# Decay and bonus tables spread by a rank-one product, a reordered first pair, and 3 KB output rows in an RWKV-5 plus soft-MoE kernel

## The chip, the core and the metric

The kernel runs on one core of a Trainium2 chip. Five engines share the work: TensorE multiplies matrices (in the profile PE, and PEld for its weight loads), VectorE (DVE) and ScalarE (ACT) work elementwise and can read what TensorE leaves in PSUM, GpSimd (POOL) works elementwise on SBUF and issues some DMAs, SyncE (SP) issues most DMAs. Each engine executes its own queue in order and waits for the others by semaphores. The metric is device time in microseconds (us), the median of several runs; lower is better. The profile covers a span about 2 us shorter than the device time.

## What is computed

Two stages, one after the other. The first is a linear attention with a decaying state, for 4 batches, 8 heads, 768 steps and head size 48; the second is a soft mixture of 8 experts with 4 slots each, over the 3072 tokens that the first produces (8 heads x 48 = 384 channels):

```python
for t in range(S):
    kt, vt, rt = (k[:, :, t], v[:, :, t], r[:, :, t])
    cur = np.einsum('bhd,bhe->bhde', u[None] * kt, vt)
    y[:, :, t] = np.einsum('bhd,bhde->bhe', rt, state + cur)
    state = w[None, :, :, None] * state + np.einsum('bhd,bhe->bhde', kt, vt)
...
logits = x @ phi                      # x: 3072 x 384, phi: 384 x 32
d = softmax of logits over tokens;  c = softmax of logits over slots
slot_out[e] = relu((d.T @ x)[e] @ w1[e]) @ w2[e]
out = c @ slot_out                    # 3072 x 384, float32
```

`w` (the decay per head and channel, 0.85 to 0.95) and `u` (the bonus for the step itself) have 8 x 48 = 384 values each.

## The kernel before

**Tiling.** The 3072 tokens are cut into 12 blocks of 256, called pairs because each holds two chunks of 128 steps. A block is loaded as `r_l`, `k_l`, `v_l`, each 128 partitions x 8 heads x 2 neighbouring steps (J = 2) x 48. Partitions 0 to 63 hold the first chunk, 64 to 127 the second. In DRAM each run of a load is 2 x 48 x 4 = 384 bytes. The pool `ld` has four buffers of each, so loads run ahead of the work, all on SP's queue, in the order k, r, v (line 70).

**The decay tables.** Within a chunk the decay is taken out of the recurrence by scaling r with `W_n = w^(step-128)` and k with `W_k = w^(127-step)`, both tables of 128 x 768 float32. Before: DMAs spread `w` and `u` over all 128 partitions (`w_rep` line 82, `u_rep` line 75; the latter sits behind the first `k_l` in SP's queue), ScalarE takes the logarithm of `w_rep` (line 122) and two exponentials (123, 124), VectorE makes the other two halves by a product with `w_rep` (125, 126). Behind these products, in VectorE's queue, stand 13 memsets of constants and of the padding of `rr` and `kk` (129 to 143). Separately `w_pd` collects `w` with channels on partitions, by two DMAs of 4-byte elements issued from ACT's queue; GpSimd squares it seven times to get `w^128` (line 148), and `tables()` spreads it into `wm`, which the state update multiplies by.

**A pair.** `mults(n)` makes `rr = r * W_n`, `kk = k * W_k` (bfloat16) and `ku = k * u` (float32): on GpSimd for n > 0; for n = 0 `ku` on GpSimd, `rr` and `kk` on VectorE (lines 191 to 193). `trans` transposes `rr` or `kk` by eight TensorE products into the single PSUM tile `t_p`, which ScalarE copies out. `att(n, j)` multiplies them to attention scores (two PSUM tiles `at_p0`, `at_p1`), VectorE masks them into `at_s` (line 261). The diagonal term is r.(u k): ScalarE copies r into the PSUM tile `rp` (`r_copy`), VectorE multiplies `ku` by it (`kur`, line 219), sums (226) and scales v (`dv`, 228); `diag` is the last two. `y_open`, `inter`, `intra` gather the output of the pair in PSUM, `state` and `st_next` advance the state, `x_copy` takes the output out. Two iterations behind, `xt`, `lg`, `expo`, `disp` compute the logits, their exponentials and the slots' inputs; every second iteration `lexp_t` transposes the exponentials into `LexpT`, and `rowsum` sums them per token into `rsum_r`. `rp` is one PSUM buffer, so the second `r_copy` of a pair waits for the first `kur`.

**Order.** It is written out by hand. Ahead of the loop (lines 405 to 415) stand `mults(0)`, the transposes of pair 0 (`rr` first), the diagonal of pair 0, and `mults(1)`. Iteration n of the loop (line 416) computes attention and state of pair n while preparing pair n + 1 and issuing `load(n + 3)` and, on GpSimd, `mults(n + 2)` and then one load of expert weights (`load_w`, 16 of 768 KB as stored; seven of them follow the last `mults`). After the loop come the experts (`up`, `down`) and the output stage (lines 501 to 517): for each of 12 blocks two products of 32 x 128 weights with 384 columns, one result scaled by VectorE and one by ScalarE into `o_s`, and one DMA. There a partition holds one row of each of two 128-token groups, so a run in DRAM is one row, 1536 bytes.

Of the kernel before, what the change touches and what calls it, by code (L numbers as in the profile page):

```python
# [11 lines left out]
def kernel(  # L12
# [12 lines left out]
    nc = tc.nc  # L25
    B, H, S, D = r.shape
    C = 128
    nC = S // C
    Nn, Dm = out.shape
    assert Nn == B * S and Dm == H * D  # L30
    ES = moe_phi.shape[1]
# [11 lines left out]
    P = 128  # L43
# [21 lines left out]
    def load(n):  # L65
        if n >= nS:
            return
        b, i = divmod(n, nSb)
        loads[n] = [ld.tile([P, H, J, D], f32, name=name) for name in ("r_l", "k_l", "v_l")]
        for x, src in ((1, k), (0, r), (2, v)):  # L70
            t = loads[n][x]
            nc.sync.dma_start(out=t[:].rearrange("p h j d -> p h (j d)"),
                              in_=src[b, :, i * TS:(i + 1) * TS, :].rearrange("h (p j) d -> p h (j d)", j=J))
            if n == 0 and x == 1:
                nc.sync.dma_start(out=u_rep[:].rearrange("p h d -> p (h d)"),
                                  in_=u.flatten().partition_broadcast(P))

    def jh(t):
        return t[:].rearrange("p h j d -> p j h d")

    w_rep = cst.tile([P, H, D], f32, name="w_rep")
    nc.sync.dma_start(out=w_rep[:].rearrange("p h d -> p (h d)"), in_=w.flatten().partition_broadcast(P))
    u_rep = cst.tile([P, H, D], f32, name="u_rep")
    w_pd = cst.tile([P, nP], f32, name="w_pd")
    nc.vector.memset(w_pd[:], 1.0)
    for par in range(2):
        nc.scalar.dma_start(out=w_pd[par * 64:par * 64 + D, :],
                            in_=w.rearrange("(q a) d -> a d q", a=2)[par])
# [6 lines left out]
    for a in range(2):  # L95
# [7 lines left out]
    row = cst.tile([P, J], f32, name="row")  # L103
    nc.vector.tensor_copy(row[:, 0:1], row_i[:])
    nc.vector.tensor_scalar_add(row[:, 1:2], row[:, 0:1], 1.0)
    ex_n = cst.tile([P, 1], f32, name="ex_n")
    nc.vector.tensor_scalar_add(ex_n[:], row[:, 0:1], float(-C))
    ex_k = cst.tile([P, 1], f32, name="ex_k")
    nc.vector.tensor_scalar(out=ex_k[:], in0=row[:, 1:2], scalar1=-1.0, scalar2=float(C - 1),
                            op0=ALU.mult, op1=ALU.add)  # L110
    col_f = cst.tile([P, J, HF], f32, name="col_f")
    nc.vector.tensor_copy(col_f[:], col_i[:])
# [2 lines left out]
        nc.vector.tensor_scalar(out=mask[:, j, :], in0=col_f[:].rearrange("p j c -> p (j c)"),  # L115
                                scalar1=row[:, j:j + 1], scalar2=None, op0=ALU.is_gt)

    W_n = cst.tile([P, J, H, D], f32, name="W_n")
    W_k = cst.tile([P, J, H, D], f32, name="W_k")
    logw = cst.tile([P, H, D], f32, name="logw")  # L120
    nc.scalar.activation(out=warm[:], in_=warm[:], func=AF.Ln)
    nc.scalar.activation(out=logw[:], in_=w_rep[:], func=AF.Ln)
    nc.scalar.activation(out=W_n[:, 0, :, :], in_=logw[:], func=AF.Exp, scale=ex_n[:])
    nc.scalar.activation(out=W_k[:, 1, :, :], in_=logw[:], func=AF.Exp, scale=ex_k[:])
    nc.vector.tensor_mul(W_n[:, 1, :, :], W_n[:, 0, :, :], w_rep[:])
    nc.vector.tensor_mul(W_k[:, 0, :, :], W_k[:, 1, :, :], w_rep[:])

    ones = cst.tile([P, P], bf, name="ones")
    nc.vector.memset(ones[:], 1.0)
    blk = cst.tile([P, G], bf, name="blk")  # L130
    nc.vector.memset(blk[:], 0.0)
    for q in range(G):
        nc.vector.memset(blk[q * ES:(q + 1) * ES, q:q + 1], 1.0)
    wm = cst.tile([P, nP, D2], f32, name="wm")
    nc.vector.memset(wm[:], 0.0)
    phi_s = cst.tile([P, nM, ES], bf, name="phi_s")
# [8 lines left out]
    st_t = [cst.tile([P, nP, D2], bf, name=f"st{i}") for i in range(2)]  # L145

    for _ in range(C.bit_length() - 1):
        nc.gpsimd.tensor_mul(w_pd[:], w_pd[:], w_pd[:])

    def tables():  # L150
        for par in range(2):
# [26 lines left out]
    with tc.tile_pool(name="wk", bufs=2) as wk, \  # L178
         tc.tile_pool(name="wk3", bufs=3) as wk3, \
         tc.tile_pool(name="ps", bufs=1, space=bass.MemoryType.PSUM) as ps:  # L180
        sc = {}

        def mults(n):
            if n >= nS:
                return
            r_l, k_l, v_l = loads[n]
            rr, kk = rr_t[n % NB], kk_t[n % NB]
            ku = wk.tile([P, J, H, D], f32, name="ku")
            u_b = u_rep[:, None, :, :].to_broadcast([P, J, H, D])
            if n == 0:  # L190
                nc.gpsimd.tensor_mul(ku[:], jh(k_l), u_b)
                nc.vector.tensor_mul(rr[:, :, :, 0:D], jh(r_l), W_n[:])  # L192
                nc.vector.tensor_mul(kk[:, :, :, 0:D], jh(k_l), W_k[:])  # L193
            else:
                nc.gpsimd.tensor_mul(rr[:, :, :, 0:D], jh(r_l), W_n[:])  # L195
                nc.gpsimd.tensor_mul(kk[:, :, :, 0:D], jh(k_l), W_k[:])  # L196
                nc.gpsimd.tensor_mul(ku[:], jh(k_l), u_b)  # L197
            sc[n] = dict(rr=rr, kk=kk, ku=ku)
# [8 lines left out]
        def r_copy(n, j):  # L207
            if n >= nS:
                return
            s = sc[n]  # L210
            if j == 0:
                s["rp"] = ps.tile([P, H, D], f32, name="rp")
            nc.scalar.copy(s["rp"][:], jh(loads[n][0])[:, j, :, :])  # L213

        def kur(n, j):
            if n >= nS:
                return
            s = sc[n]
            nc.vector.tensor_mul(s["ku"][:, j, :, :], s["ku"][:, j, :, :], s["rp"][:])  # L219

        def diag(n):
            if n >= nS:
                return
            s = sc[n]
            d = s["rp"][:].rearrange("p h d -> p (h d)")[:, 0:J * H].rearrange("p (j h) -> p j h", j=J)
            nc.vector.tensor_reduce(d, s["ku"][:], axis=mybir.AxisListType.X, op=ALU.add)  # L226
            dv = wk.tile([P, J, H, D], bf, name="dv")
            nc.vector.tensor_mul(dv[:], s["v"][:], d[:, :, :, None].to_broadcast([P, J, H, D]))  # L228
            s["dv"] = dv

        def trans(n, nm):
            if n >= nS:
                return
            s = sc[n]
            t_p = ps.tile([P, nP, 2, J, HF], bf, name="t_p")
            for q in range(nP):
                for j in range(J):
                    nc.tensor.transpose(t_p[:, q, :, j, :],  # L238
                                        s[nm][:, j, 2 * q:2 * q + 2, :].rearrange("p h d -> p (h d)"), ident[:])
            t_s = wk.tile([P, nP, 2, J, HF], bf, name=f"t_{nm}")  # L240
            nc.scalar.copy(t_s[:], t_p[:])  # L241
            s["t_" + nm] = t_s
# [149 lines left out]
        def lexp_t(g):  # L392
            le_p = ps.tile([P, P + 2 * G], bf, name="le_p", tag="xl_p", padded_shape=[P, XW + 4 * ES])
            lt_of[g] = le_p
            nc.tensor.transpose(le_p[:, 0:P], le_of[g][:].rearrange("p g s -> p (g s)"), ident[:])
            nc.scalar.copy(LexpT[:, g, :].rearrange("s (p j) -> s j p", j=J),
                           le_p[:, 0:P].rearrange("s (j p) -> s j p", j=J))

        def rowsum(g):
            rs_p = lt_of.pop(g)[:, P:P + 2 * G].bitcast(f32)  # L400
            nc.tensor.matmul(rs_p, LexpT[:, g, :], blk[:], start=True, stop=True, skip_group_check=True)
            nc.vector.reciprocal(rsum_r[:, g * G:(g + 1) * G], rs_p)

        W_AT = [1, 1, 1, 1, 1, 1, 1, 1, 1, 1, 2, 2, 1, 1]
        mults(0)
        trans(0, "rr")
        r_copy(0, 0)
        trans(0, "kk")
        v_cast(0)
        tables()  # L410
        kur(0, 0)
        r_copy(0, 1)
        kur(0, 1)
        diag(0)
        mults(1)
        for n in range(nS + 2):
            live = n < nS
            load(n + 3)
            group = (n - 3) // 2 if n >= 3 and n % 2 == 1 else None
            att(n, 0)  # L420
            mults(n + 2)
            s_now = ps.tile([P, nP * D2], f32, name="s_p")
            disp(n - 2, s_now)
# [74 lines left out]
                                soT[:, mi, :, :].rearrange("p g s -> p (g s)"), ident[:])  # L498
        nc.vector.tensor_copy(so_r[:], sr_p[:])

    out_ap = out.rearrange("(no p) m -> p no m", p=P)
    with tc.tile_pool(name="ob", bufs=6) as ob, \
         tc.tile_pool(name="out_ps", bufs=2, space=bass.MemoryType.PSUM) as out_ps:
        for g in range(nG):
            for jj in range(0, G, 2):
                o_s = ob.tile([P, 2, Dm], f32, name="o_s")
                for j in (jj, jj + 1):
                    o_p = out_ps.tile([P, Dm], f32, name=f"o_p{j}")
                    nc.tensor.matmul(o_p[:], LexpT[j * ES:(j + 1) * ES, g, :], so_r[j * ES:(j + 1) * ES, :],  # L509
                                     tile_position=(j * ES, 0))  # L510
                    ni = g * G + j
                    if j % 2 == 0:
                        nc.vector.tensor_scalar_mul(o_s[:, 0, :], o_p[:], rsum_r[:, ni:ni + 1])
                    else:
                        nc.scalar.activation(out=o_s[:, 1, :], in_=o_p[:], func=AF.Copy,  # L515
                                             scale=rsum_r[:, ni:ni + 1])
                nc.sync.dma_start(out=out_ap[:, g * G + jj:g * G + jj + 2, :], in_=o_s[:])


# [28 lines left out]
```

The softmax here doesn't subtract the row's maximum and nothing guards it: scores larger than these inputs give would overflow.

## Time and profile before

Device time 147.52 us (median of 3 runs, 147.45 to 148.28); the profiled span is 145.3 us. The stages, as the table of stretches and the order of instructions give them:

| stretch, us | what runs | length, us |
|---|---|---|
| 0 to 20.47 | loads, tables, first pair, until VectorE masks the first scores | 20.5 |
| 20.47 to 105.4 | the first 11 of the 12 iterations, each from one masking of `att(n, 0)` to the next | 84.9 |
| 105.4 to 116.7 | the last iteration, logits and slots of the last pairs | 11.3 |
| 116.7 to 128.3 | the experts | 11.6 |
| 128.3 to 145.3 | output | 17.0 |

Over the whole span VectorE and TensorE are busy 66%, GpSimd 54%, ScalarE 52%. Such shares average stages with different limits, so they say little about what an edit at the start or at the end is worth; the views by stage in the prediction say more.

How to read the lines there: a line of the order of instructions (the timeline) gives start, length, engine, source line, operation, output <- inputs, shape and count, and in brackets the idle time of the engine just ahead and what ended it. A line of stretches gives the stretch, its length, each engine's busy time and count of instructions, the TensorE clock that was granted, the mean busy share of the 16 DMA engines (transfers that overlap can bring it above 1) and GB/s moved. SPq, ACTq are the queues that issue DMAs.

### The profile page before, as it was taken

To read this page: it belongs to the slowest core of one execution; us is meant where nothing else is said; L and a number is where in the kernel's file an instruction comes from. 1 tells how busy PE (TensorE), PEld (TensorE's weight loads), DVE (VectorE), ACT (ScalarE), POOL (GpSimd) and SP (SyncE) were. 2 spreads that over 40 slices of the span, in tenths; PEclk is the share of its full clock that TensorE was granted. 3 is DMA by queue.
4 is the path that set the end of the run, shared out by engine and by line. 5 is a ranking of instruction groups with operands and counts; after the bars stand their busy time and mean duration, and the time that the engine had idled before them with its cause. 6 is when DMAs were issued, how large, how long until landed. Compare 5 with 4: busy or idle time off the path is not lost.

```text
span 145.3 us, 4488 instructions
## 1 busy us (share of the span) xinstructions
PE 95.6 (66%) x1927; PEld 73.2 (50%) x1927; DVE 96.0 (66%) x191; ACT 75.4 (52%) x123; POOL 77.9 (54%) x67
## 2 busy tenths in 40 slices
PE   0004509998858996858489994799767489977000
PEld 0004306777636865646357873676646289931000
DVE  3095197979888679998988688868980223267600
ACT  4713833657776648584958277763914300046500
POOL 5195999895998398999591899940000000000000
PEclk9999999999995559999975589555995555555555
DMA  3999999999999999999999949699999990009995
GB/s 58 230 301 324 321 320 312 185 261 206 306 240 241 238 262 228 228 287 229 252 234 239 260 55 196 98 201 210 205 208 208 206 188 11 5 26 361 367 362 189
DMA packets 52980, 32.19 MB, mean 221 GB/s; under 512 B 38352, under 2 KB 49872, under 8 KB 52960
## 3 DMA queue, kind: packets, MB, share of 16 engines
q0 software_dynamic: 11552, 12.63, 52.7%
q1 hardware_dynamic: 40992, 19.27, 47.1%
q8 instruction: 15, 0.25, 0.6%
q10 hardware_dynamic: 416, 0.00, 0.2%
q14 instruction: 5, 0.04, 0.1%
HBM read 39.77 MB, written 4.72 MB: 306 GB/s over the span
## 4 chain that ended last, share of the span: by engine, by line
PE 34%; DVE 22%; ACT 19%; DMA 13%; issue 7%; SPq 0%; ACTq 0%; DVEq 0%
DVE at_s L261 11%; PE at_p L256 6%; DMA out_dram<-o_s 5%; DMA r_l<-in_r_dram 5%; ACT t_kk L241 4%; DVE ku L219 4%; PE t_p L238 4%; PE h_p L470 4%; ACT xt_s L346 4%; PE so_p L482 4%; PE xl_p L344 3%; PE s_p L301 3%; ACT v_bf L204 3%; DMA w_rep<-in_w_dram 3%; ACT x_t L330 2%
## 5 line engine op out<-in xcount | busy, mean ns | idle before, releaser
L261 DVE TENSOR_TENSOR at_s<-at_p,mask 128x512 bf16<-128x512 f32 x48 | 30.9, 686 | 10.0 <-PE at_p L256 9.9
L196 POOL TENSOR_TENSOR kk<-k_l,W_k 128x768 bf16<-128x768 f32 x11 | 19.9, 1810 | 11.3 <-PE s_p L301 10.7
L195 POOL TENSOR_TENSOR rr<-r_l,W_n 128x768 bf16<-128x768 f32 x11 | 20.0, 1821 | 1.9 <-DVE kk L193 1.7
L241 ACT COPY t_rr<-t_p 128x1024 bf16<-128x1024 bf16 x12 | 12.1, 1012 | 16.1 <-PE t_p L238 16.1
L197 POOL TENSOR_TENSOR ku<-k_l,u_rep 128x768 f32<-128x768 f32 x11 | 20.0, 1816 | 0.0
L256 PE MATMUL at_p<-t_rr,t_kk 64*64 64x128 bf16 x384 | 15.0, 264 | 7.3 <-DVE at_s L261 6.2
L213 ACT COPY rp<-r_l 128x384 f32<-128x384 f32 x24 | 11.6, 485 | 15.2 <-DVE ku L219 13.6
L238 PE MATMUL t_p<-ident,rr 128*128 128x128 bf16 x96 | 9.8, 263 | 11.8 <-DVE rr L192 11.8
L219 DVE TENSOR_TENSOR ku<-ku,rp 128x384 f32<-128x384 f32 x24 | 13.2, 550 | 5.5 <-ACT rp L213 4.9
L515 ACT ACTIVATE o_s<-o_p,rsum_r 128x384 f32<-128x384 f32 x12 | 6.4, 585 | 16.3 <-PE o_p L509 13.8
L256 PEld LDWEIGHTS <-t_kk 64*64 64x64 bf16 x384 | 9.3, 128 | 10.7 <-issue 8.1
L176 POOL DMA_DIRECT2D w_all<-in_moe_w_dram x16 | 13.6, 854 | 0.0
L238 PEld LDWEIGHTS <-rr 128*128 128x128 bf16 x96 | 7.3, 118 | 12.1 <-DVE rr L192 11.8
L301 PE MATMUL s_p<-v_bf,kk 64*128 64x96 bf16 x160 | 13.3, 240 | 0.0
L301 PEld LDWEIGHTS <-kk 64*128 64x128 bf16 x160 | 9.7, 113 | 5.8 <-issue 5.8
L241 ACT COPY t_kk<-t_p 128x1024 bf16<-128x1024 bf16 x12 | 12.1, 1006 | 0.9 <-PE t_p L238 0.7
L228 DVE TENSOR_TENSOR dv<-v_bf,rp 128x768 bf16<-128x768 bf16 x12 | 11.4, 954 | 1.2
L310 DVE TENSOR_TENSOR st<-s_p,wm 128x384 bf16<-128x384 f32 x20 | 11.1, 553 | 1.7 <-PE s_p L301 1.5
L330 ACT CAST x_t<-y_p 128x768 bf16<-128x768 f32 x12 | 9.7, 805 | 4.5 <-PE y_p L323 4.3
L226 DVE TENSOR_REDUCE rp<-ku 128x16 f32<-128x768 f32 x12 | 11.5, 958 | 0.3
L346 ACT COPY xt_s<-xl_p 128x768 bf16<-128x768 bf16 x12 | 9.6, 800 | 3.7 <-PE xl_p L344 3.6
L238 PE MATMUL t_p<-ident,kk 128*128 128x128 bf16 x96 | 9.9, 265 | 1.1 <-ACT t_rr L241 1.1
(78 smaller groups left out, 175.7 us busy)
## 6 DMA issues: line engine op xcount, KB each, us to landing
w_all<-in_moe_w_dram POOLq DMA_DIRECT2D x16, 768.0 KB, 10.1
k_l<-in_k_dram SPq DMA_DIRECT2D x12, 384.0 KB, 6.7
r_l<-in_r_dram SPq DMA_DIRECT2D x12, 384.0 KB, 8.0
v_l<-in_v_dram SPq DMA_DIRECT2D x12, 384.0 KB, 7.4
out_dram<-o_s SPq DMA_DIRECT2D x12, 384.0 KB, 4.1
w_rep<-in_w_dram SPq DMA_DIRECT2D x1, 192.0 KB, 3.9
u_rep<-in_u_dram SPq DMA_DIRECT2D x1, 192.0 KB, 6.0
phi_f<-in_moe_phi_dram POOLq DMA_DIRECT2D x1, 48.0 KB, 5.9
```

The lines of the kernel that those rows point to most:

```text
L176: nc.gpsimd.dma_start(out=dst[:, e, :, :], in_=src[:, e, :, :])
L195: nc.gpsimd.tensor_mul(rr[:, :, :, 0:D], jh(r_l), W_n[:])
L196: nc.gpsimd.tensor_mul(kk[:, :, :, 0:D], jh(k_l), W_k[:])
L197: nc.gpsimd.tensor_mul(ku[:], jh(k_l), u_b)
L219: nc.vector.tensor_mul(s["ku"][:, j, :, :], s["ku"][:, j, :, :], s["rp"][:])
L238: nc.tensor.transpose(t_p[:, q, :, j, :], s[nm][:, j, 2 * q:2 * q + 2, :].rearrange("p h d -> p (h d)"), ident[:])
L241: nc.scalar.copy(t_s[:], t_p[:])
L256: nc.tensor.matmul(at_p[a][g * HF:(g + 1) * HF, q, :], kT[sl, q, g, j, :], rT[sl, q, g, :, :].rearrange("p j c -> p (j c)"), start=True, s ...
L261: nc.vector.tensor_mul(s["at"][:, a, j, :, :], at_p[a][:], mask[:, j, None, :].to_broadcast([P, nP, P]))
L301: nc.tensor.matmul(s_p[:, q * D2:(q + 1) * D2], s["kk"][sl, j, 2 * q:2 * q + 2, :].rearrange("p h d -> p (h d)"), s["v"][sl, j, 2 * q:2 * ...
L330: nc.scalar.copy(x_t[:], sc[n]["y"][:, :, 0:Dm])
L346: nc.scalar.copy(xt_s[:], xl_p[:, 0:XW])
```

## The change

Four groups of edits, shortened to their core:

1. **Tables.** `w` and `u` come as one row each (1.5 KB) instead of 128 copies. The logarithm is taken of one row; a product with a row of ones on TensorE (float32, contraction length 1) spreads log w and u over the partitions, into the PSUM buffers that `att` uses later. All four halves of the tables are exponentials read from PSUM, `W_k` first; VectorE copies `u_rep` from PSUM. The products of lines 125 and 126 are gone, and the memsets no longer stand behind them.
2. **First pair.** VectorE makes `kk`, `rr` and `ku` of pair 0, in this order; the squarings of `w_pd` move from GpSimd to VectorE, ahead of them. k is transposed first. Pair 0 has a PSUM buffer of its own for the first r copy, so both copies can go early. The sum of the diagonal comes ahead of the transposes, its product with v (`dmul`) after the first `att`. `mults(1)` is put into GpSimd's queue ahead of the transposes.
3. **Row sums.** `LexpT` keeps the even and odd steps apart; `rowsum` becomes four small products.
4. **Output.** A partition holds two neighbouring tokens, so a run in DRAM is 3 KB; a block takes four products of 32 x 64 weights instead of two of 32 x 128.

```diff
-            if n == 0 and x == 1:
-                nc.sync.dma_start(out=u_rep[:].rearrange("p h d -> p (h d)"),
-                                  in_=u.flatten().partition_broadcast(P))
...
-    w_rep = cst.tile([P, H, D], f32, name="w_rep")
-    nc.sync.dma_start(out=w_rep[:].rearrange("p h d -> p (h d)"), in_=w.flatten().partition_broadcast(P))
+    wu_row = cst.tile([1, 2, Dm], f32, name="wu_row")
+    for t, src in enumerate((w, u)):
+        nc.sync.dma_start(out=wu_row[:, t, :], in_=src.flatten()[None, :])
...
-    nc.scalar.activation(out=logw[:], in_=w_rep[:], func=AF.Ln)
-    nc.scalar.activation(out=W_n[:, 0, :, :], in_=logw[:], func=AF.Exp, scale=ex_n[:])
-    nc.scalar.activation(out=W_k[:, 1, :, :], in_=logw[:], func=AF.Exp, scale=ex_k[:])
-    nc.vector.tensor_mul(W_n[:, 1, :, :], W_n[:, 0, :, :], w_rep[:])
-    nc.vector.tensor_mul(W_k[:, 0, :, :], W_k[:, 1, :, :], w_rep[:])
...
     for _ in range(C.bit_length() - 1):
-        nc.gpsimd.tensor_mul(w_pd[:], w_pd[:], w_pd[:])
+        nc.vector.tensor_mul(w_pd[:], w_pd[:], w_pd[:])
...
+        nc.scalar.activation(out=logw[:], in_=wu_row[:, 0, :], func=AF.Ln)
+        lw_p = ps.tile([P, Dm], f32, name="lw_p", tag="at_p0", padded_shape=[P, nP * P])
+        u_p = ps.tile([P, Dm], f32, name="u_p", tag="at_p1", padded_shape=[P, nP * P])
+        nc.tensor.matmul(u_p[:], ones_f[:], wu_row[:, 1, :], start=True, stop=True)
+        nc.tensor.matmul(lw_p[:], ones_f[:], logw[:], start=True, stop=True)
+        for Wt, ex in ((W_k, ex_k), (W_n, ex_n)):
+            for j in range(J):
+                nc.scalar.activation(out=Wt[:, j, :, :].rearrange("p h d -> p (h d)"), in_=lw_p[:], func=AF.Exp,
+                                     scale=ex[:, j:j + 1])
+        nc.vector.tensor_copy(u_rep[:].rearrange("p h d -> p (h d)"), u_p[:])
...
             if n == 0:
-                nc.gpsimd.tensor_mul(ku[:], jh(k_l), u_b)
+                nc.vector.tensor_mul(kk[:, :, :, 0:D], jh(k_l), W_k[:])
                 nc.vector.tensor_mul(rr[:, :, :, 0:D], jh(r_l), W_n[:])
-                nc.vector.tensor_mul(kk[:, :, :, 0:D], jh(k_l), W_k[:])
+                nc.vector.tensor_mul(ku[:], jh(k_l), u_b)
...
-            nc.tensor.matmul(rs_p, LexpT[:, g, :], blk[:], start=True, stop=True, skip_group_check=True)
+            for q2 in range(2):
+                for j in range(J):
+                    nc.tensor.matmul(rs_p[q2 * HF:(q2 + 1) * HF, 2 * j:2 * j + 2],
+                                     LexpT[:, g, j * HF:(j + 1) * HF], blk[:, q2, :],
+                                     start=True, stop=True, tile_position=(0, q2 * HF), skip_group_check=True)
...
         mults(0)
+        r_copy(0, 0)
+        r_copy(0, 1)
+        kur(0, 0)
+        kur(0, 1)
+        dsum(0)
+        mults(1)
+        trans(0, "kk")
         trans(0, "rr")
-        r_copy(0, 0)
-        trans(0, "kk")
         v_cast(0)
         tables()
-        kur(0, 0)
-        r_copy(0, 1)
-        kur(0, 1)
-        diag(0)
-        mults(1)
...
             att(n, 0)
+            if n == 0:
+                dmul(0)
             mults(n + 2)
...
-    out_ap = out.rearrange("(no p) m -> p no m", p=P)
+    out_ap = out.rearrange("(i p j) m -> i p j m", p=P, j=J)
...
-                    nc.tensor.matmul(o_p[:], LexpT[j * ES:(j + 1) * ES, g, :], so_r[j * ES:(j + 1) * ES, :],
-                                     tile_position=(j * ES, 0))
+                for q2 in range(2):
+                    q = 2 * qh + q2
+                    nc.tensor.matmul(o_p[q2 * HF:(q2 + 1) * HF, :],
+                                     LexpT[q * ES:(q + 1) * ES, g, j * HF:(j + 1) * HF],
+                                     so_r[q * ES:(q + 1) * ES, :],
+                                     tile_position=(q * ES, q2 * HF), skip_group_check=True)
```

## The prediction

> **What bounds the kernel now.** I read three views: the order of instructions at the start, the stretches of the loop, and the output stage.
>
> The start, to the first masking of scores on VectorE:
>
> ```profile
> 0.74 0.39 SPq L82 DMA_DIRECT2D w_rep<-in_w_dram  x1
> ...
> 4.69 0.52 ACT L122 ACTIVATE logw<-w_rep 128x384 f32<-128x384 f32 x1 [1.38 <-DMA w_rep<-in_w_dram]
> 5.23 1.28 ACT L123 ACT_TABLE_LOAD   x1
> ...
> 6.72 2.41 POOL L148 TENSOR_TENSOR w_pd<-w_pd 128x4 f32<-128x4 f32 x7 [3.88 <-DMA w_pd<-in_w_dram]
> 7.18 0.56 DVE L125 TENSOR_TENSOR W_n<-W_n,w_rep 128x384 f32<-128x384 f32 x1 [4.81 <-ACT W_n L123]
> ...
> 9.07 1.81 POOL L191 TENSOR_TENSOR ku<-k_l,u_rep 128x768 f32<-128x768 f32 x1
> ...
> 10.06 1.64 DVE L192 TENSOR_TENSOR rr<-r_l,W_n 128x768 bf16<-128x768 f32 x1
> 11.63 0.95 DVE L193 TENSOR_TENSOR kk<-k_l,W_k 128x768 bf16<-128x768 f32 x1
> ...
> 12.59 1.81 POOL L195 TENSOR_TENSOR rr<-r_l,W_n 128x768 bf16<-128x768 f32 x1 [1.71 <-DVE kk L193]
> ...
> 18.01 0.55 DVE L219 TENSOR_TENSOR ku<-ku,rp 128x384 f32<-128x384 f32 x1 [3.13 <-ACT rp L213]
> ...
> 20.47 1.28 DVE L261 TENSOR_TENSOR at_s<-at_p,mask 128x512 bf16<-128x512 f32 x2
> ```
>
> VectorE sits idle 4.8 us until the tables, then does 13 memsets (8.2 to 10.1), and scales r before k. Pair 0's scores exist at 16.6, but their masking waits until 20.47: the second r copy stands behind four ScalarE operations (17.50), and the diagonal behind it. GpSimd begins pair 1 at 12.59 because r_l of pair 1, issued at 7.69, took 4.8 us to land (the DMA view); the releaser named is a guess.
>
> The loop:
>
> ```profile
> 58.50:65.70 7.20, 5.12 (x127) 3.97 (x124) 6.24 (x12) 5.33 (x10) 7.18 (x5) 1.00 1.20 258
> ...
> 72.90:82.00 9.10, 8.39 (x133) 6.38 (x133) 6.80 (x13) 5.60 (x10) 5.47 (x4) 0.58 1.17 237
> 82.00:89.40 7.40, 5.57 (x124) 4.31 (x122) 6.17 (x10) 5.07 (x9) 7.38 (x6) 0.82 0.85 150
> ```
>
> Columns: stretch, length, busy time of PE, PEld, DVE, ACT, POOL, clock, DMA share, GB/s. At full clock an iteration lasts 7.2 us with VectorE busy 6.2; at half clock PE takes over (8.4 of 9.1). This happens in three iterations (8.8, 9.1, 8.5). The loop hangs on engines, not loads: the r_l of pair 11 lands at 84.0, yet its transpose runs near 98.5. So a start x earlier should move the loop by x, while loads keep up.
>
> The output:
>
> ```profile
> 132.00:134.00 2.00, 1.18 (x6) 0.20 (x4) 1.38 (x3) 1.17 (x3) 0.00 (x0) 0.50 1.00 363
> 134.00:136.00 2.00, 0.50 (x2) 0.10 (x1) 1.06 (x2) 1.05 (x2) 0.00 (x0) 0.50 1.00 363
> ```
>
> DMA is full (share 1.00, 363 GB/s), the engines have time: 12 x 393 KB at 363 GB/s is 13.0 of the 17 us.
>
> [...] No float32 product is in this trace. [...] The 1536-byte packets here gave 363 GB/s. [...]
>
> **Part by part.**
>
> *DMA ahead of the loads.* Removed: 2 x 196 KB. k_l landed at 7.1 (1.19 + 5.9), r_l at 8.9, v_l at 10.1, then one per 1.2 us. In the new order k_l is issued about 1.6, with two 1.5 KB rows ahead. w_rep's transfer began about 1 us after issue, 393 KB at 300 GB/s takes 1.3, landing adds 1: k_l about 5.0, r_l 6.2, v_l 7.5, pair 1's k_l 8.7, r_l 9.9. Gain 2.1 to 2.7 us; certainly over 1.2, the removed bytes at 320 GB/s.
>
> *Tables.* The rows land about 2.2 us after issue (the smallest DMA time in the trace is 2.5; bounds 1.8 and 4), w at 2.9. The logarithm follows the table load and warm-up (3.31) and lasts 0.52: 3.8. TensorE makes u first. [...] u from 3.3 to 4.8, log w to 6.3. The second table load (1.28) hides beside them. Four exponentials of 0.6 (L123): W_k ready at 7.5, W_n at 8.7 (bounds 5.5 and 10).
>
> *VectorE before kk.* The memsets (about 2 us) now lie in its idle time, before 5. The squarings add a wait: w_pd landed at 6.54, now with less traffic 5.3 to 6.5, then seven dependent operations of 0.15 (row L105), 1.05; then the u copy, 0.5 (VectorE's 384-column rows: 0.36 to 0.62). Everything of pair 0 on VectorE is queued behind that wait, and TensorE waits for kk. Free at 6.9 to 8.1; kk starts at 7.8. On GpSimd nothing useful goes away: 4.2 us lay before 12.59 anyway.
>
> *Pair 0.* kk 7.8 to 8.75, rr to 9.7, ku to 10.65 (0.95 each, L193). [...] Two kur at 0.55 and the sum at 0.96, as before: VectorE free at 13.0. Meanwhile: k transposes 8.75 to 9.8 (8 in 1.03), copy to 10.8 (1.01); t_p is one buffer, so r's transposes follow, to 11.9, copy to 13.0; att 0.64, scores at 13.6. Masking starts at 13.9 instead of 20.47: 6.6 us. The product dmul (0.95), formerly ahead of it, now stands behind: the second masking comes at 13.9 + 1.28 + 0.95 = 16.1 instead of 22.48. Gain 6.3 us. [...]
>
> *Carried through the loop?* GpSimd is only 2 to 2.5 us earlier: pair 1 from 10.6 to 16.0, pair 2 to 21.4 (3 x 1.81 each). ku of pair 2 is needed at 23.7 - 6.3 + 7.3 = 24.7: in time. It needs 3 x 1.81 + 0.8 = 6.2 us of an iteration of 7.2. Loads gain 2.4, not 6.3, as DMA is full (share over 1.0) to 84; their lead of over 10 us shrinks by 4. The last expert load lands at 120.9 and is used about 126.5. Loads have 1.7 us of DMA work less, and the dip of 82 to 89.4 (share 0.85, 150 GB/s) holds some 3 us; GpSimd issues the tail's seven loads after its last pair, so the last lands about 117 against a need at 120.2. So all 6.3 are carried; a half-clock iteration more or less is 1.3 to 1.9 either way.
>
> *Row sums.* 18 more products of 0.2 us over six groups, mostly in gaps of PE; the last group stands before the experts: +0.1. Unstrided LexpT copy: under 0.05, nothing.
>
> *Output.* [...] I take 0.2. The first block needs two more products: +0.1. Later ones hide behind the DMA: evictions take 0.62 of 1.08 per block.
>
> Sum: -6.3 + 0.1 - 0.2 + 0.1 = -6.3; 147.5 - 6.3 = 141.2 us.
>
> **Rivals.**
>
> [...]
>
> *DMA sets the end.* If loads or the expert tail move only with the removed bytes (2.4 us), 145.1. For it: DMA shares over 1.0. Against: the dip and the 5.6 us of slack.
>
> *Output gains more, or a half-clock phase goes:* 139.
>
> [...]
>
> **How the numbers follow.** Forecast 0.55, part lost 0.22, more 0.12, DMA 0.08, slower 0.03. Time: 141.2. The range leaves out the slow case, most of the DMA case and the edges: 138.3 to 144.3. Within 1% means 146.0 to 149.0: only mixtures of the DMA case and a worse start, 0.04. Slower 0.03, faster 0.93.
>
> **What would show it.** r_l of pair 1 landing near 9.9; W_k from 6.3 to 7.5; VectorE's kk at 7.8 and not behind w_pd past 8.1; first masking near 13.9; iterations of 7.2 to 9.1 as before; the experts 6.3 us earlier, without a wait for their weights; output DMA at 363 to 375 GB/s. Wrong it would be if the iterations lengthened to the DMA's pace, if the float32 products took over 2 us each, or if PE showed up as the releaser of every output eviction.

## The result and the profile after

Device time fell from 147.8 us (4 runs, 147.45 to 148.28) to **140.91 us** (4 runs, 140.58 to 142.17): a ratio of 0.955, 95% interval 0.948 to 0.961. The profiled span fell from 145.3 to 139.2 us. On another chip the same kernel gave 142.48 us beside 147.58 (ratio 0.962, 0.956 to 0.968). Single runs on some chips were disturbed; the ratios leave them out, the medians don't, and two kernels below (the old order and the combined one) were profiled in such a run, so that little but their start is read.

The 6.17 us of span, by stage; a stage ends where the next begins, and minus means shorter:

| stage ends with | before, us | after, us | this stage alone |
|---|---|---|---|
| first masking on VectorE | 20.47 | 13.00 | -7.47 |
| masking of the last pair (loop) | 105.40 | 97.42 | -0.51 |
| slots of all tokens done | 116.61 | 108.69 | +0.06 |
| experts' result (`so_r`) | 128.33 | 122.57 | **+2.16** |
| end | 145.34 | 139.17 | -0.41 |

So the start gave 7.5 us and the loop kept it. The experts lost 2.2 us, and the output gave 0.4.

The start, from the order of instructions of the kernel after:

```profile
3.04 1.61 PE L180 MATMUL u_p<-wu_row,ones_f 1*128 1x384 f32 x2 [3.04 <-DMA wu_row<-in_u_dram]
...
3.75 1.28 ACT L184 ACT_TABLE_LOAD   x1
...
4.26 1.29 DVE L138 TENSOR_TENSOR w_pd<-w_pd 128x4 f32<-128x4 f32 x7
4.45 1.48 PE L181 MATMUL lw_p<-logw,ones_f 1*128 1x384 f32 x2
...
5.97 1.05 ACT L184 ACTIVATE W_k<-lw_p,ex_k 128x384 f32<-128x384 f32 x2 [0.94 <-PE lw_p L181]
...
7.05 0.96 DVE L196 TENSOR_TENSOR kk<-k_l,W_k 128x768 bf16<-128x768 f32 x1 [1.04 <-ACT W_k L184]
...
8.87 0.95 DVE L198 TENSOR_TENSOR ku<-k_l,u_rep 128x768 f32<-128x768 f32 x1
...
10.43 1.80 POOL L200 TENSOR_TENSOR rr<-r_l,W_n 128x768 bf16<-128x768 f32 x1 [7.51 <-DMA r_l<-in_r_dram]
...
12.32 0.64 PE L274 MATMUL at_p<-t_rr,t_kk 64*64 64x128 bf16 x16 [1.10 <-ACT t_rr L259]
...
13.00 1.29 DVE L279 TENSOR_TENSOR at_s<-at_p,mask 128x512 bf16<-128x512 f32 x2 [1.06 <-PE at_p L274]
```

`kk` starts at 7.05 instead of 11.63, and the bracket names what holds it now: the exponentials of W_k, not the squarings (over at 5.55) or `k_l` (landed at 5.07). The masking now waits for the scores themselves (`<-PE at_p`); before, it stood in VectorE's queue behind the diagonal. The reads of `t_kk` and `t_rr` out of `t_p` and the scores form a chain of TensorE and ScalarE alone.

The loop and the output, as stretches (columns as before: stretch, length, busy PE, PEld, DVE, ACT, POOL, clock, DMA share, GB/s):

```profile
27.75:34.94 7.19, 4.82 (x121) 3.80 (x122) 6.17 (x10) 5.14 (x9) 7.15 (x6) 1.00 1.15 262
34.94:43.68 8.74, 7.97 (x130) 6.12 (x130) 6.76 (x12) 5.42 (x10) 8.72 (x6) 0.55 1.23 250
...
81.27:90.00 8.73, 8.26 (x130) 6.35 (x130) 6.76 (x12) 5.35 (x9) 7.69 (x6) 0.50 0.87 140
...
130.00:132.00 2.00, 0.00 (x0) 0.00 (x0) 1.28 (x3) 1.21 (x3) 0.00 (x0) 0.50 1.01 397
```

Eight of the eleven iterations last 7.2 to 7.5 us and three, at a clock of 0.50 to 0.61, 8.1 to 8.7; before, there were three such too, of 8.5 to 9.1. The last line is new: a full DMA moves 397 GB/s at the output, where it moved 363.

The experts:

```profile
113.32 0.78 PE L493 MATMUL h_p<-unsiT,w_all 128*128 128x4 bf16 x24
...
113.96 0.78 PE L505 MATMUL so_p<-hT,w_all 128*128 128x4 bf16 x24
...
114.60 0.25 PE L493 MATMUL h_p<-unsiT,w_all 128*128 128x4 bf16 x4
...
116.53 0.69 PE L493 MATMUL h_p<-unsiT,w_all 128*128 128x4 bf16 x20 [1.68 <-issue]
...
119.64 0.46 PE L505 MATMUL so_p<-hT,w_all 128*128 128x4 bf16 x12
120.25 1.12 PE L505 MATMUL so_p<-hT,w_all 128*128 128x4 bf16 x36 [0.16 <-issue]
```

The 24 products of a layer follow at 0.027 us each (0.64 us from one layer to the next). In the sixth expert TensorE stops after 4 of 24, and again 128 products later, after 12 of 24. The brackets name no engine and no DMA: `issue` is time in which the profile shows nothing that the engine waits for. Counted from where the next product was due (114.60 + 4 x 0.027 = 114.71, and 119.64 + 12 x 0.027 = 119.96), the holes are 1.82 and 0.29 us: together 2.1 of the 2.16 us lost. The loss varies: in a second profile of the same kernel (experiment 6) the holes stand at the same places and come to 1.84 and 1.12 us, and the experts took 14.72 us instead of 13.88. The last expert weights landed at 118.33, so a wait for data was the first suspect.

### The profile page after: what moved, and what is told of

Same layout as the page of the kernel before. It is cut to its first block, busy times and chain, and to the rows that moved or that the text cites. A ratio compares the mean times of both kernels' runs of the same rounds, so it can differ in the third digit from the quotient of the medians.

```text
span 139.2 us, 4595 instructions
## 1 busy us (share of the span) xinstructions
PE 101.7 (73%) x1973; PEld 77.1 (55%) x1973; DVE 96.6 (69%) x199; ACT 76.1 (55%) x125; POOL 74.2 (53%) x59
## 4 chain that ended last, share of the span: by engine, by line
PE 42%; ACT 21%; DVE 18%; issue 8%; DMA 6%; SPq 0%; ACTq 0%; DVEq 0%
DVE at_s L279 10%; PE at_p L274 6%; PE t_p L256 6%; ACT t_kk L259 5%; DMA out_dram<-o_s 5%; PE h_p L493 4%; PE xl_p L362 4%; DVE ku L228 4%; PE so_p L505 4%; ACT xt_s L364 4%; PE s_p L319 3%; ACT v_bf L209 3%; ACT x_t L348 3%; PE y_p L341 2%; ACT rp L222 2%
## 5 line engine op out<-in xcount | busy, mean ns | idle before, releaser
L200 POOL TENSOR_TENSOR rr<-r_l,W_n 128x768 bf16<-128x768 f32 x11 | 19.9, 1813 | 18.5 <-DMA r_l<-in_r_dram 18.4
L228 DVE TENSOR_TENSOR ku<-ku,rp 128x384 f32<-128x384 f32 x23 | 12.6, 548 | 0.7
L256 PE MATMUL t_p<-ident,kk 128*128 128x128 bf16 x96 | 10.4, 273 | 2.1 <-DVE kk L196 2.1
L239 DVE TENSOR_REDUCE rp<-ku 128x16 f32<-128x768 f32 x12 | 11.5, 958 | 0.3
L256 PEld LDWEIGHTS <-kk 128*128 128x128 bf16 x96 | 7.7, 123 | 4.6 <-DVE kk L196 3.3
```

The costliest lines, as they stand in the source:

```text
L256: nc.tensor.transpose(t_p[:, q, :, j, :], s[nm][:, j, 2 * q:2 * q + 2, :].rearrange("p h d -> p (h d)"), ident[:])
```

## Experiments

The edits are shown in short; some lines only name what changes.

**1. Which group pays: the start alone, and the output alone.** The first kernel has groups 1 and 2 with the old row sums and output; the second has groups 3 and 4 on the start of before.

```diff
 # start alone: the kernel after with (in words)
+rs_p = LexpT[:, g, :] x blk              (one product per group, not four)
+out_ap = out.rearrange("(no p) m -> p no m", p=P)     (1536-byte runs)
```

> Groups 1 and 2 of the change alone; row sums and output as before. Theory: the start carries the whole gain up to the experts (first masking at 13.0 as in the changed kernel against 20.5 before, logits done 7.9 us earlier), and the experts then lose up to 2.2 us to a stall, so 139.6 to 141.8 us; the output stage lasts 17.0 us at 363 GB/s. Rival: the 3 KB rows earn a good part of the 6.9 us, then this kernel stays at 143 or above.

> Groups 3 and 4 of the change alone; start as before. Theory: the output DMA runs at 397 instead of 363 GB/s, 1.1 us less of transfer, of which 0.4 to 0.8 is lost because the first block is issued later; first masking at 20.5; 146.7 to 147.3 us. Rival: the rows are worth their full 1.1 us or more, 146.4 or below, or the four small products per block hold the DMA back, 148 or above.

The start alone took 143.06 us (beside 147.07; ratio 0.967, 0.953 to 0.981), with the first masking at 12.71. The output alone took 146.9 us (ratio 1.002, 0.997 to 1.006): its output stage was 0.42 us shorter, 16.59 instead of 17.01, but this is 0.3% and disappears in the interval of the whole. The gain is that of the start.

The total of the start alone lies where the rival expected it (143 or above), but not for the rival's reason: the start gave 7.8 us, as the theory has it, and the experts lost 4.3, not up to 2.2.

The start alone showed more of the experts (16.02 us instead of 11.72):

```profile
113.68 0.73 PE L490 MATMUL h_p<-unsiT,w_all 128*128 128x4 bf16 x22
115.99 0.21 PE L490 MATMUL h_p<-unsiT,w_all 128*128 128x4 bf16 x2 [1.58 <-issue]
...
121.79 0.80 PE L502 MATMUL so_p<-hT,w_all 128*128 128x4 bf16 x24 [2.38 <-DMA w_all<-in_moe_w_dram]
```

The first stop now comes after 22 of 24 products, not after 4. This kernel executes 18 products fewer ahead of the experts (one row-sum product instead of four in each of six groups), and the stop stands exactly 18 products later in the stream. The stop belongs to a place in TensorE's instruction stream, not to a weight. The second stop here is another thing: a true wait for data, as the last expert's weights landed at 121.75.

**2. The tables' transport, and the order, apart.** One kernel keeps the new order but spreads `w` and `u` by two DMAs as before; the other keeps the new tables but puts pair 0, the squarings and `mults(1)` in the old order.

```diff
 # transport by DMA
-nc.sync.dma_start(out=wu_row[:, t, :], in_=src.flatten()[None, :])
+nc.sync.dma_start(out=w_rep, in_=w.flatten().partition_broadcast(P))     (and u_rep)
 # old order
-kk, rr, ku on VectorE;  r_copy x2, kur x2, dsum, mults(1), trans kk, trans rr
+ku on GpSimd, rr, kk on VectorE;  trans rr, r_copy, trans kk, kur, r_copy, kur, diag, mults(1)
```

> The changed kernel, but w and u are again spread over the partitions by two DMAs of 196 KB at their old places in the queue; the log is taken of all partitions and the exponentials read SBUF. All order edits stay. Theory A (the order of the start carries the gain): k_l lands at 7.1 and W_k is ready at 7.7, so the first masking comes at 13.8 to 14.5, a loss of 0.8 to 1.5 us against the changed kernel. Theory B (the lighter DMA carries it): 15.5 or later, 2.5 us or more lost.

> The changed kernel with its tables by a rank-one product and its early memsets, but pair 0 as before: ku of pair 0 and the squarings on GpSimd, r first, one r buffer, the diagonal after the transposes. Theory A (order): the tables are ready at 8, but the first masking waits for the second r copy and the diagonal, at 16 to 18. Theory B (DMA and tables): below 15, most of the 7.5 us stays.

The old order took 144.14 us (ratio 0.983, 0.975 to 0.991). Its start:

```profile
7.71 0.96 DVE L197 TENSOR_TENSOR rr<-r_l,W_n 128x768 bf16<-128x768 f32 x1 [2.69 <-ACT W_n L184]
...
14.98 0.56 DVE L224 TENSOR_TENSOR ku<-ku,rp 128x384 f32<-128x384 f32 x1 [3.13 <-ACT rp L218]
...
17.44 1.28 DVE L275 TENSOR_TENSOR at_s<-at_p,mask 128x512 bf16<-128x512 f32 x2
```

The scores were there at 13.61 (12.97 + 0.64), yet VectorE waited 3.13 us for the second r copy and masked at 17.44. `k_l` and `r_l` landed at 5.04 and 6.47, as in the kernel after. So with the new tables in place the order, with the moves between engines and the second r buffer that belong to it, is worth 17.44 - 13.00 = 4.4 us, and the rest of the start (transport, table arithmetic, memsets out of the way; not taken apart) 20.47 - 17.44 = 3.0 us.

The transport by DMA took 143.44 us (ratio 0.978, 0.970 to 0.986):

```profile
6.58 1.34 DVE L138 TENSOR_TENSOR w_pd<-w_pd 128x4 f32<-128x4 f32 x7 [1.98 <-DMA w_pd<-in_w_dram]
...
7.84 0.96 DVE L191 TENSOR_TENSOR kk<-k_l,W_k 128x768 bf16<-128x768 f32 x1
...
9.38 0.96 DVE L192 TENSOR_TENSOR rr<-r_l,W_n 128x768 bf16<-128x768 f32 x1 [0.58 <-DMA r_l<-in_r_dram]
...
12.97 1.80 POOL L195 TENSOR_TENSOR rr<-r_l,W_n 128x768 bf16<-128x768 f32 x1 [10.16 <-DMA r_l<-in_r_dram]
...
13.98 1.29 DVE L274 TENSOR_TENSOR at_s<-at_p,mask 128x512 bf16<-128x512 f32 x2 [0.67 <-PE at_p L269]
```

Here the tables are not what is waited for last (W_k is ready at 6.48 + 1.12 = 7.60). `w_pd` and the loads behind the broadcasts are: the squarings start 2.3 us later than in the kernel after, `rr` waits for `r_l`, GpSimd gets pair 1's `r_l` at 12.97 instead of 10.43. At the first masking that costs 1.0 us, at the next pair's 2.1 (22.45 instead of 20.35). Its total is not a clean measure of this: the clock phases gave the loop back 1.2 us (83.2 us for eleven periods, 84.4 after), and its experts took 16.32 us. Their first stop bears out what the start alone showed. This kernel leaves out the two rank-one products, four records in the trace, and stops four products later than the kernel after, after 8 of 24:

```profile
114.29 0.35 PE L488 MATMUL h_p<-unsiT,w_all 128*128 128x4 bf16 x8
116.60 0.56 PE L488 MATMUL h_p<-unsiT,w_all 128*128 128x4 bf16 x16 [1.96 <-issue]
```

**3. What stops the experts.** If the weights' data are late, experts that read weights already in place don't stop; if the instructions are late, they do. Two kernels: experts 4 to 7 read the weights of 0 to 3 while all loads still run; and the same without the last seven loads.

```diff
-w1_all[:, e, mi, ...]   w2_all[:, e, fi, ...]
+w1_all[:, e % 4, mi, ...]   w2_all[:, e % 4, fi, ...]
 # second kernel, also
+w_todo = w_todo[:9]
```

> The changed kernel, except that experts 4 to 7 compute with the weights of experts 0 to 3, which landed some 50 us earlier; all 16 loads still run. It asks what the 1.7 us stop of TensorE in the middle of an expert is. Theory A (instructions): TensorE's own instructions come by DMA in blocks of 16 KB, and such a block is held up by the expert loads; the stop stays, 1 to 2 us, in the middle of an expert, with no releaser named. Theory B (data): it waits for expert weights; it is gone and the experts last 11.7 us as before.

> As the run above, and the last seven of the 16 expert loads are left out, so DMA is idle in the experts' stretch. Theory A and B both: no stop over 0.3 us, experts of 11.7 us or less, and 138.5 to 139.5 us. If a stop of over 1 us stayed, it would be neither weights nor traffic.

With early weights and all loads (143.63 us, a single run; the experts took 15.99), TensorE's instructions:

```profile
115.16 0.25 PE L493 MATMUL h_p<-unsiT,w_all 128*128 128x4 bf16 x4
117.00 0.69 PE L493 MATMUL h_p<-unsiT,w_all 128*128 128x4 bf16 x20 [1.60 <-issue]
...
120.12 0.46 PE L505 MATMUL so_p<-hT,w_all 128*128 128x4 bf16 x12
122.92 1.12 PE L505 MATMUL so_p<-hT,w_all 128*128 128x4 bf16 x36 [2.35 <-issue]
```

The same two places, with no load to wait for. Without the tail's loads (137.39 us; ratio 0.934, 0.926 to 0.943), the waits of VectorE for the experts' first products (`h_p`) are those of the kernel before again. The first line is of the kernel before, the second of the kernel after, the others of this one:

```profile
DVE hT L475 <- PE h_p L470: 4.0, 8, 1.0
...
DVE hT L498 <- PE h_p L493: 5.8, 8, 2.3
...
DVE hT L499 <- PE h_p L494: 4.0, 8, 1.0
DVE soT L509 <- PE so_p L506: 3.6, 8, 0.4
```

(in total, times, longest). No stop is left, and the experts take 11.72 us, to the digit what they took before the change. The total fell by more than these 2.2 us, and below the 138.5 to 139.5 expected; the rest lies ahead of the experts, whose first product came at 107.59 instead of 108.84. So the data are not the cause of the stops, and the loads' traffic is. The page of the kernel after shows what else goes by DMA beside the loads:

```profile
q0 software_dynamic: 11552, 12.63, 55.1%
...
q8 instruction: 15, 0.25, 0.6%
```

15 packets of 0.25 MB in all are 16 KB each. Without the tail's loads, three of these packets are all that the DMA moved from 107 to 119 us. I take q8 to be TensorE's queue, and one packet to bring what TensorE executes from one stop to the next. The stops lie 128 products apart, which with their 128 weight loads are 256 instructions; and TensorE executes 1973 products and 1973 weight loads in the span, 263 for each packet, where VectorE, the next, executes 199 instructions in all. This is a reading of counts; no view names the engine that a packet is for. I call such 256 instructions a block. The packets in the trace, beside the time at which TensorE entered the block before (worked out from the experts' first product and 0.027 us per product, in us):

| kernel | block before entered | packet starts (after) | packet ends | next block due | it starts | hole |
|---|---|---|---|---|---|---|
| after, 1st | 111.30 | 114.29 (3.0) | 115.26 | 114.71 | 116.53 | 1.8 |
| after, 2nd | 116.53 | 117.73 (1.2) | 118.70 | 119.94 | 120.25 | 0.3 |
| early weights, 1st | 111.85 | 114.71 (2.9) | 115.67 | 115.26 | 117.00 | 1.7 |
| early weights, 2nd | 117.00 | 120.60 (3.6) | 121.50 | 120.41 | 122.92 | 2.5 |
| no tail loads, 1st | 110.05 | 110.48 (0.4) | 111.44 | 113.46 | in time | 0 |
| no tail loads, 2nd | 113.46 | 114.48 (1.0) | 115.43 | 116.87 | in time | 0 |

The experts use up a block in 3.41 us. With no loads beside it a block is moved and usable within some 2.7 to 3.3 us of entering the block before, by estimate (0.4 to 1.0 to the packet's start, 1.0 for the packet, and 1.3 from its end to the first instruction, as at the first stop), just in time. Behind the weight loads the packet started 2.9 to 3.6 us after, three times of four, and TensorE ran dry. The margin is thin (3.41 against 2.7 to 3.3 us): in the old order, whose last weights had landed at 119.28, a packet of 1.27 us still left a hole of 0.30 us at 125.18. Why the packet starts 3 us late, and what the last 1.3 to 1.6 us are, the trace does not show.

**4. The tail's loads earlier.** If traffic beside the experts is the cause, fewer loads left for the end must shrink the stops. The dip at 81 to 90 us (140 GB/s) has room: iteration 8 issues three loads instead of one, which leaves five for the tail.

```diff
-W_AT = [1, 1, 1, 1, 1, 1, 1, 1, 1, 1, 2, 2, 1, 1]
+W_AT = [1, 1, 1, 1, 1, 1, 1, 1, 3, 1, 2, 2, 1, 1]
```

> The changed kernel with two of the seven tail loads of expert weights issued one iteration earlier, ahead of the last mults on GpSimd, into the stretch of 81 to 90 us where DMA moved 140 GB/s. Theory (DMA sets the experts' end): the last weights land at 113 to 116 instead of 118.3 to 122, no wait for them is left, the stop for instructions shrinks to 0 to 1.2 us; 139.3 to 140.5 us. Rival (the loads were never the limit): no change against 140.9, or slower because the loads of pairs 10 and 11 come late.

```profile
114.67 0.25 PE L493 MATMUL h_p<-unsiT,w_all 128*128 128x4 bf16 x4
115.77 0.70 PE L493 MATMUL h_p<-unsiT,w_all 128*128 128x4 bf16 x20 [0.86 <-issue]
...
118.89 1.46 PE L505 MATMUL so_p<-hT,w_all 128*128 128x4 bf16 x48
```

140.76 us (beside 147.61), with runs from 139.03 to 141.85: the total, forecast at 139.3 to 140.5, shows no gain over the kernel after; the stage does. In the profile (span 138.1) the last load landed at 114.75 instead of 118.33, the first stop halved, the second is gone, and the experts took 12.78 us instead of 13.88.

Profiles of other kernels fall into the same order, by and large: the longer loads still land after the slots are done, the longer the experts take.

| kernel | last load after the slots, us | experts, us |
|---|---|---|
| before | 4.3 | 11.7 |
| early tail | 6.0 | 12.8 |
| after | 9.6 | 13.9 |
| after, second profile | 11.5 | 14.7 |
| transport by DMA | 13.9 | 16.3 |
| start alone (a wait for data among it) | 14.0 | 16.0 |

**5. The length of the output's runs.** Everything as after, but a partition holds tokens 128 apart again: four products, 1536-byte runs. Only the output's row order changes.

```diff
-out.rearrange("(i p j) m -> i p j m", p=P, j=J)
+out.rearrange("(i j p) m -> i p j m", p=P, j=J)
```

> The changed kernel with one row of DRAM per run again in the output DMA (1536 bytes; each DMA still covers one block of 256 tokens, the two rows of a partition 128 rows apart, so the rows of a block come out in another order). Theory A: the length of the run sets the rate: 363 GB/s instead of 397, output stage 1.1 us longer. Theory B: the rate comes from something else in the change: 397 GB/s stays.

```profile
128.00:130.00 2.00, 1.55 (x10) 0.36 (x7) 1.07 (x3) 1.00 (x3) 0.00 (x0) 0.50 1.00 363
130.00:132.00 2.00, 0.38 (x4) 0.00 (x0) 1.17 (x2) 1.08 (x2) 0.00 (x0) 0.50 1.00 361
```

The rate is back at 361 to 363 GB/s with the products unchanged, so the run length makes the difference here. The output stage took 17.28 us instead of 16.60, 0.7 longer (1.1 was forecast). The whole took 143.51 us (ratio 0.968, 0.959 to 0.976), but of the 1.6 us between the two profiles the other 0.9 stand ahead of the output, where the kernels are the same: the slots were done 0.5 us later and the experts took 0.4 us more.

**6. The order within the first pair, and a version that combines.** One kernel scales and transposes r first; one makes log w's product before u's, copies u only ahead of `ku`, and has the early tail of 4; beside them runs the kernel after, unedited.

```diff
 # r first
-kk, rr, ku ... trans(0, "kk"); trans(0, "rr")
+rr, kk, ku ... trans(0, "rr"); trans(0, "kk")
 # log w first
-matmul(u_p, ...); matmul(lw_p, ...)
+matmul(lw_p, ...); matmul(u_p, ...)
```

> The changed kernel with rr of pair 0 scaled and transposed ahead of kk again; the tables keep their order, W_k first. Theory: rr has to wait for W_n (7.95) where kk waited for W_k (7.05), and both transposes are needed, so the first masking is 0.9 us later, 13.5 to 13.9. Rival: k first is worth 2 us or more, 15 or later.

> Both improvements that the runs point to: two tail loads of expert weights earlier, and the product that spreads log w ahead of the one that spreads u (the u copy then ahead of ku). Theory: W_k was the last thing that kk waited for, behind 0.7 us of the u product; kk starts at 6.3 to 6.5 instead of 7.05, the first masking at 12.0 to 12.4, and the experts lose 1 us less; 138.8 to 139.8 us, 1 to 2 us under the changed kernel. Rival: r_l, which lands at 6.5, or the early loads take the place of what was removed; no difference.

> The changed kernel unedited, as the measure for the other two on the same chip: 140.5 to 142 us.

With r first (141.7 us, a single run) VectorE waits for W_n and the first masking comes at 13.69, against 13.00 and 12.71 in the two profiles of the kernel after:

```profile
7.74 0.96 DVE L196 TENSOR_TENSOR rr<-r_l,W_n 128x768 bf16<-128x768 f32 x1 [1.47 <-ACT W_n L184]
...
13.69 1.29 DVE L279 TENSOR_TENSOR at_s<-at_p,mask 128x512 bf16<-128x512 f32 x2 [1.14 <-PE at_p L274]
```

k first is worth 0.7 to 1.0 us there, with W_k the first table made in both. With log w first, the wait ahead of `kk` is as long as before but ends sooner:

```profile
6.55 0.96 DVE L195 TENSOR_TENSOR kk<-k_l,W_k 128x768 bf16<-128x768 f32 x1 [1.01 <-ACT W_k L184]
...
12.50 1.29 DVE L279 TENSOR_TENSOR at_s<-at_p,mask 128x512 bf16<-128x512 f32 x2 [0.47 <-PE at_p L274]
```

`kk` starts 0.5 us earlier and the masking 0.2 to 0.5; 12.0 to 12.4 was expected for it. The combined kernel took 140.32 us (ratio to before 0.952, 0.947 to 0.957; 138.8 to 139.8 us expected) beside 142.48 for the kernel after on the same chip (0.962, 0.956 to 0.968). These intervals touch, and the kernel after had 0.955 in its first measurement, so a lead is not shown. Nor is the early tail borne out here: in this profile, whose loop ended 3.6 us later than that of the kernel after, the last weights landed 11.5 us after the slots were done and both stops stand (1.75 and 0.84 us).

## Why the prediction was right, and where not

The forecast of 141.2 us was met within 0.3 us, and that close by luck: the start gave 1.2 us more than the 6.3 of the sum, the loop and the output together 0.8 more, and the experts took 2.2 back, which the sum had at nothing.

- **DMA ahead of the loads: right.** `k_l` landed at 5.07 (5.0 said), `r_l` 6.49 (6.2), `v_l` 7.89 (7.5), pair 1's `k_l` 9.08 (8.7).
- **Tables: right.** log w was spread at 5.93 (6.3), W_k ready at 7.02 (7.5). The float32 products took 1.61 (u) and 1.48 us (log w). No run shows where the prediction's 1.5 us for each (u from 3.3 to 4.8, log w to 6.3) comes from; it was the author's estimate, and near. The exponentials took 0.525 instead of 0.6, and the second table load (3.75 to 5.03) hid beside the products (3.04 to 5.93).
- **Squarings: right that they don't hold `kk`, with `w_pd` mis-sized.** It landed at 3.54, 2.2 us after issue; 5.3 to 6.5 was forecast from a trace in which it crossed the broadcasts. With these back (experiment 2) the squarings start at 6.58.
- **Pair 0: right in kind, 0.9 us too careful.** The first masking came at 13.00, not 13.9: `kk` began 0.75 earlier. And the 13.0 at which VectorE was to be free holds 0.3 us beyond the lengths named there (10.65 + 2 x 0.55 + 0.96 is 12.7), which no run shows: `ku` took 0.95 us and ended at 9.82, before GpSimd began at 10.43, and VectorE was free at 11.94. `rr`, which took 1.64 us in the kernel before, beside GpSimd's `ku`, took 0.96 with GpSimd idle.
- **Carried through the loop: right.** 7.5 us at the first masking, 7.4 at the second, 7.9 when the slots were done; the three half-clock iterations sum to 25.6 us instead of 26.4. GpSimd waits 18.4 us in six waits for `r_l` in the groups of the page, and no iteration lengthens.
- **Row sums: right.** The last group's four products took 0.27 us instead of 0.18, its stage 0.06 more (0.1 said).
- **A stop in the experts, put at nothing ("so the last lands about 117 against a need at 120.2. So all 6.3 are carried"), is the step that failed.** The sum compared the last load's landing (117 said, 118.33 measured) with its need, and found slack. The landing was near, and the data didn't stall. But the traffic of these loads now lay beside the experts, which ran 7.9 us earlier while the last load came only 2.5 us earlier, and the packets of TensorE's instructions started late, three times of four 2.9 to 3.6 us after the block before was entered (experiment 3). In the kernel before, the first block fetched in the experts went out at 120.22, as the loads ended (120.87), and caused no stop. The prediction weighed the loads only by when their data land; the term was 0 and measured +2.2.
- **Output: right in direction, too small.** No run shows where the sum's 0.2 us for the longer runs, and the 375 GB/s that it looked for at most, come from; the rate rose by 9%, 363 to 397 GB/s. A 1536-byte packet took 67 to 68 ns on average, one of 3072 bytes 123 to 124; from the first packet to the last it was 12.42 us instead of 13.22. The first block's head gave some back: from `so_r` to the first issue 1.67 us instead of 1.33. Net -0.4 instead of -0.1.

Of the rivals, "DMA sets the end" was wrong in its mechanism for the kernel as changed, but a true wait for the last weights (2.38 us) did appear in the start alone. The case of a start partly lost (0.22) did not come: the start gave 7.5 us. Nor did that of a slower kernel (0.03): in the output stage the DMA stayed full (share 1.01, 397 GB/s).

## What to carry to other kernels

When an earlier stage gets faster, ask not only whether a later stage's data still arrive in time, but what traffic that stage now runs beside: the many tiny products of the experts used up a block of instructions in 3.41 us, about as fast as one came (2.7 to 3.3 us with no load beside it, by estimate), and a stop at `issue` at a fixed place of the instruction stream, with a packet of the `instruction` queue that starts late, was the sign here. At a start, look for short results that stand behind long ones in one queue; here the order of ready work was worth more (4.4 us) than the rest of the start's edits (3.0). A gain of some tenths at the output is real in its stage and invisible in the total; read it in the stage.

## What the runs showed of the hardware

- Packets of 16 KB on the `instruction` queue, by the counts TensorE's (15 of them to 3946 products and weight loads): in the experts, with no load under way, a packet started 0.4 to 1.0 us after TensorE entered the block before, and TensorE didn't stop. Beside 768 KB loads it started 2.9 to 3.6 us after, three times of four, and TensorE stopped for 1.7 to 2.5 us each time.
- At the output a packet of 1536 bytes took 67 to 68 ns and one of 3072 bytes 123 to 124, and the rate was 363 and 397 GB/s on one core.
- The transfer of 4-byte elements (`w_pd`, 0.8 KB) landed 2.1 us after its issue (the median of its two DMAs), and 4.5 us after once two broadcasts ran beside it (experiment 2).
